# A fused attention and gated-MLP kernel: SyncE's transfers in the attention stage in written order, with new due times for the row maxima

## The chip, the cores and the metric

One Trainium2 chip, one NeuronCore of it. The metric is the device time of one execution in microseconds (us), as the median of several runs. The core has a matrix engine (TensorE, called PE in the profile, with its weight loads as PEld), two elementwise engines (VectorE, DVE; ScalarE, ACT), a slower general engine (GpSimd, POOL), and SyncE (SP), which here does nothing but issue DMA transfers. SBUF is the on-chip memory, PSUM holds matmul results, and DRAM tensors are off the core.

## The reference

`x` is 2048 by 576. Its normalised form goes through sliding-window attention (32 heads of 18, each query sees itself and the 255 keys before it); `x` itself goes through a gated MLP of width 4608 whose gate mixes positions by a 2048 by 2048 matrix.

```
def reference(x, wqkv, wo, x, w_in, w_sp, b_sp, w_out):
    qkv = layernorm(x) @ wqkv
    p = softmax(where(0 <= i - j < 256, q @ k.T * 18 ** -0.5, -1e9))
    s = (p @ v) @ wo
    z = gelu(x @ w_in);  z1 = z[:, :2304];  z2 = layernorm(z[:, 2304:])
    y = z1 * (w_sp @ z2 + b_sp[:, None])
    return x + s * silu(y @ w_out)
```

## The kernel before

Precision is kept by splitting a float32 operand into a high part (float32r) and the rest, and by multiplying three pairs of parts; most matmuls of the kernel are such triples.

The program has five stages, one after the other on PE. It normalises and transposes `x` and forms q and k (line 291). It forms v (458) and z2 (662). Then comes the attention stage, which this change concerns. After it follow the projection by `wo` (839), the mixing by `w_sp` (1029) and the output matmuls (1101).

The attention stage works in 16 units: 8 groups of four heads, first for the lower half of the queries (units 0 to 7), then for the upper half (units 8 to 15), which also see 256 keys of the lower half. Three kinds of work are interleaved on PE. First, `scores` (508) computes transposed scores of unit u, ACT takes the exponential (512), POOL cuts the window's edges (516, 519), and `pv` (532) multiplies by v, whose extra column of ones gives the softmax denominator. Second, `row_max` computes the row maxima of unit u+1, and of the first rows of unit u+2: a matmul (387) into one of two PSUM buffers `sp`, and a DVE instruction pair (391) that adds the window mask and reduces to the maximum. The maxima of a unit are written to DRAM (405) and read back as two more rows of q (409), so that the matmul for the scores subtracts them. Third, `z1_matmuls` (438) computes z1, which has nothing to do with attention and fills the gaps; its results go to DRAM by way of ACT (441) and a store (443), and each of its 18 weight blocks is loaded (416) and split by ACT and DVE (447) ahead of use.

`finish` ends a unit. The 4 by 1024 denominators are read out of `ou` into a 128 by 32 tile (`den`, 581), inverted on DVE (554), written to DRAM (556), read back spread over 32 rows for each head (`rp`, 559), and `ou` is multiplied by `rp` on DVE in two halves (567) and stored (576). So between the end of a unit and its store there is a chain: transfer, DVE, transfer, transfer, DVE, transfer.

The q and k of two heads share one slot tile of SBUF (`att0` to `att4`). `load_pair` fills a slot with eight transfers (346 to 349); at the start of unit u the pair for heads 2 and 3 of unit u+1 and the pair for heads 0 and 1 of unit u+2 are loaded. A row-maximum matmul reads the whole slot, so it needs all eight.

The order of the work is written out by a planner in the program itself. It keeps a running sum of estimated durations, `clock` (`spend`), and an estimate of when ACT and DVE come free (`use`, `busy`). `due` holds times at which each score block and each row maximum should be issued, as shares of the unit's length; where nothing is due, a z1 matmul is issued (`fill`). `after(ns, fn)` calls `fn` once the clock has gone on by `ns`; with it the planner places the steps of `finish`. `tc.manual_schedule` names the engines whose instructions run in exactly this order: before, PE, POOL, DVE and ACT in the attention stage. SP was not among them: the order of its transfers was chosen by the library's scheduler from dependences and its own time estimates. Whoever chooses it, SP issues in a fixed order: a transfer that waits holds back those behind it.

## Time and profile before

| what | value |
|---|---|
| median of 3 runs | 1983.74 us (1982.5 to 1984.1) |
| profiled execution | 1989.0 us |
| its span, first to last instruction | 1987.3 us |
| PE busy over the span | 1936.0 us, 97% |
| DVE / ACT / POOL busy | 1056.9 / 899.5 / 284.7 us |
| attention stage | about 448 to 987 us of the span |
| granted PE clock, mean | 0.995 |

All durations below come from the one profiled execution; the sum is made against its span. A busy PE in the profile means that a matmul is in the pipeline, so short gaps between matmuls do not show as idle; a stretch that does show as idle is a real halt of the stage, since PE works through its instructions in order. "Idle before, releaser" tells how long an engine had stood still ahead of an instruction and what ended it.

### The profile page before, as it was taken

Reading aid. Unit: us, or ns where it says so; the run is one execution under the profiler, and the core shown is the slowest. Engines: PE = TensorE matmul, PEld = TensorE weight load, DVE = VectorE, ACT = ScalarE, POOL = GpSimd, SP = SyncE. Lnnn points to the kernel's source line nnn. Section 1 sums busy time; section 2 is a strip of 40 time slices with the busy share of each in tenths; the row PEclk is TensorE's granted clock in tenths of the full one; section 3 lists DMA queues with packets and bytes.
Section 4 is the critical chain, followed back from the end, with each engine's and each line's share of the span. In section 5 each row is a group of like instructions: output and inputs, shape, how many; then the busy total and the mean of one; then the engine's idle time right before and its main releaser. Section 6 shows DMA issues by size and latency. Waiting matters only on the chain.

```text
span 1987.3 us, 30748 instructions
## 1 busy us (share of the span) xinstructions
PE 1936.0 (97%) x11096; PEld 1654.7 (83%) x11096; DVE 1056.9 (53%) x2294; ACT 899.5 (45%) x1673; POOL 284.7 (14%) x360
## 2 busy tenths in 40 slices
PE   6999999999999999999899999999999999999998
PEld 5889999996777777777697887788888888899998
DVE  6511233366666665655225768656876567653222
ACT  4222222215555555556546655655555534442121
POOL 5000365103222223223200000000000000000000
PEclk9999999999999999999999999999999999999999
DMA  8656799424455555454566757766667555865441
GB/s 248 174 146 170 253 344 338 173 82 138 130 153 147 155 140 153 138 149 112 159 224 219 249 187 257 270 212 217 217 224 258 178 181 183 266 211 164 138 147 56
DMA packets 221368, 375.58 MB, mean 189 GB/s; under 512 B 43296, under 2 KB 118176, under 8 KB 221088
## 3 DMA queue, kind: packets, MB, share of 16 engines
q1 hardware_dynamic: 205856, 349.66, 56.7%
q10 hardware_dynamic: 15360, 23.97, 3.3%
q8 instruction: 87, 1.43, 0.3%
q14 instruction: 65, 0.53, 0.1%
HBM read 260.45 MB, written 112.83 MB: 188 GB/s over the span
## 4 chain that ended last, share of the span: by engine, by line
PE 81%; DMA 10%; DVE 5%; issue 2%; ACT 1%; POOL 1%; SPq 0%; ACTq 0%; DVEq 0%; POOLq 0%
PE acc L1029 28%; PE po L1101 11%; PE mm L438 9%; PE mm L662 9%; PE mm L291 6%; PE sp L387 4%; PE ops L532 4%; PE tps L508 4%; PE wops L839 3%; PE vps L458 3%; DMA att<-st_d 2%; DMA z1t<-z_d 1%; DMA den<-ou 1%; DMA spr<-in_w_sp_dram 1%; DVE spl L112 1%
## 5 line engine op out<-in xcount | busy, mean ns | idle before, releaser
L1029 PE MATMUL acc<-spl,zh 128*128 128x512 f32 x1008 | 393.6, 390 | 2.9 <-DVE spl L112 2.7
L1029 PE MATMUL acc<-sph,zh 128*128 128x512 f32 x1008 | 393.3, 390 | 3.0 <-ACT sph L111 2.9
L1029 PE MATMUL acc<-sph,zl 128*128 128x512 f32 x1008 | 392.8, 390 | 0.0
L391 DVE CUSTOM_DVE_ANT_0 junk<-sp,band 128x384 bf16<-128x384 f32 (+1 forms) x512 | 269.1, 537 | 174.1 <-PE sp L387 168.1
L512 ACT ACTIVATE pt<-tps 128x384 f32<-128x384 f32 (+2 forms) x576 | 244.6, 438 | 191.5 <-PE tps L508 181.4
L438 PE MATMUL mm<-b,z1wh 128*128 128x512 f32 x648 | 236.0, 395 | 0.0
L1029 PEld LDWEIGHTS acc<-spl,zh 128*128 128x128 f32 x1008 | 189.6, 188 | 44.9 <-DVE spl L112 5.6
L1029 PEld LDWEIGHTS acc<-sph,zh 128*128 128x128 f32 x1008 | 189.5, 188 | 43.6 <-ACT sph L111 4.2
L112 DVE TENSOR_TENSOR spl<-spr,sph 128x1024 fp32r<-128x1024 f32 x168 | 205.3, 1222 | 36.6 <-ACT sph L111 35.5
L1029 PEld LDWEIGHTS acc<-sph,zl 128*128 128x128 f32 x1008 | 189.6, 188 | 39.2
L662 PE MATMUL mm<-z2wh,b 128*128 128x384 f32 x720 | 192.6, 337 | 2.2 <-ACT zt L672 2.2
L508 PE MATMUL tps<-att 128*128 128x384 f32 (+1 forms) x576 | 180.7, 324 | 8.7 <-ACT pt L512 8.7
L111 ACT ACTIVATE zh<-b 128x384 fp32r<-128x384 f32 x168 | 87.4, 520 | 221.6 <-PE acc L1029 221.5
L387 PE MATMUL sp<-att 128*128 128x384 f32 (+1 forms) x512 | 178.3, 354 | 8.1 <-DVE mx L391 4.1
L111 ACT ACTIVATE sph<-spr 128x1024 fp32r<-128x1024 f32 x168 | 175.9, 1047 | 6.4 <-DMA spr<-in_w_sp_dram 4.8
L112 DVE TENSOR_TENSOR zl<-b,zh 128x384 fp32r<-128x384 f32 x168 | 93.1, 554 | 148.2 <-ACT zh L111 147.8
L1101 PE MATMUL po<-b,yh 128*128 128x288 f32 x840 | 146.4, 296 | 0.0
L387 PEld LDWEIGHTS sp<-att 128*128 128x128 f32 x512 | 95.0, 188 | 61.6 <-issue 26.0
L438 PE MATMUL mm<-b,z1wl 128*128 128x512 f32 x360 | 142.4, 396 | 0.0
L673 DVE BATCH_NORM_STATS2 st<-zt 128x6 f32<-128x384 f32 x96 | 53.5, 559 | 166.1 <-ACT zt L672 166.0
L662 PE MATMUL mm<-z2wl,b 128*128 128x384 f32 x400 | 134.3, 336 | 0.0
L662 PEld LDWEIGHTS mm<-z2wh,b 128*128 128x128 f32 x720 | 131.4, 189 | 3.3 <-ACT zt L672 3.3
(154 smaller groups left out, 2852.9 us busy)
## 6 DMA issues: line engine op xcount, KB each, us to landing
spr<-sc_d SPq DMA_DIRECT2D x96, 512.0 KB
spr<-in_w_sp_dram SPq DMA_DIRECT2D x72, 512.0 KB
zr<-z_d SPq DMA_DIRECT2D x144, 192.0 KB
st_d<-qkhl SPq DMA_DIRECT2D x72, 256.0 KB
z_d<-zt ACTq DMA_DIRECT2D x48, 384.0 KB
z_d<-z1o SPq DMA_DIRECT2D x72, 256.0 KB
z1t<-z_d SPq DMA_DIRECT2D x72, 256.0 KB
y_d<-z1t SPq DMA_DIRECT2D x72, 256.0 KB
```

What stands on the lines that cost most here:

```text
L111: act.activation(hi, src, AF.Copy)
L112: dve.tensor_tensor(lo, src, f32(hi), ALU.subtract)
L291: pe.matmul(ps, w, r, start=n == 0, stop=n == len(pl) - 1)
L387: pe.matmul(ps[:, :w], q_of(u, j)[:, i * P:(i + 1) * P], k_of(u, j)[:, k0:k0 + w], start=True, stop=True)
L391: dve.tensor_tensor_reduce(out=junk[:, :w], in0=ps[:, :w], in1=band[:, m0:m0 + w], scale=1.0, scalar=-3.0e38, op0=ALU.add, op1=ALU.max, ac ...
L438: pe.matmul(ps, w, r, start=n == 0, stop=n == len(pl) - 1)
L508: pe.matmul(ps[:, :m * P], k_of(u, j)[:, (kb - base) * P:(kb - base + 1) * P], q_of(u, j)[:, (a - lo) * P:(a - lo + m) * P], start=True, s ...
L512: act.activation(pt[:, j, d0:d0 + n * P], ps[:, (qa - a) * P:(qa - a + n) * P], AF.Exp, scale=scale)
L532: pe.matmul(o_ps[c][32 * j:32 * j + 32, (lo - 4 * c) * P:(hi - 4 * c + 1) * P], vgs[u][:, kb - k0, j * VW:j * VW + 32], pt[:, j, (lo - kb) ...
L662: pe.matmul(ps[:, :ZW], r, wt, start=n == 0, stop=n == len(pl) - 1)
L1029: pe.matmul(acc[j], z[:, ps], w[:, cs], start=s == i == 0 and n in OPENS, stop=s == 7 and i == 2, skip_group_check=True)
L1101: pe.matmul(po[i][:, a, :288], y if ahead else y[:, i * P:(i + 1) * P], w[:, a * 288:(a + 1) * 288], start=f == 0 and m == 0, stop=f == NF ...
```

## The change

SP joins the engines in written order within the attention stage, and so every transfer there is now placed by the planner's clock:

- The sixteen transfers of the two pairs are issued one by one, 450 ns of the clock apart, from 300 ns after the start of the unit (in unit 0 4 us later). `load_pair` at once is still used ahead of attention.
- The steps of `finish`: `den` is read 300 ns after ACT's copy by the planner's account (before: 700 ns after the call); the reciprocal comes 5.5 us after the call (10 us); the write of the inverse follows it by 300 ns and the read of `rp` by another 2.7 us (before: at once, in this order); the first half is multiplied at 13.5 us (22.5), the second at 20.5 us (24.5), and the four stores follow 400 ns apart.
- The two transfers of the row maxima are placed 400 ns and 3 us after DVE's account is done; z1's store 200 ns after ACT's copy; z1's next weight block is loaded at the first matmul of a block instead of the fourteenth.
- Due times: the first 16 row maxima of a unit are spread up to 0.30 of its length and the others from 0.31 to 0.765 (before: all evenly to 0.74); 7 instead of 6 of the unit after next are taken in advance, from 0.81 on (0.78).
- Unit 0 gets a share of z1 matmuls of 24 against 18 (18.4 in the upper half), its scores and maxima are due 4 us later, and POOL clears both new slots, where DVE cleared one.
- The five blocks of `wo` pass through three buffers instead of two, and are split five score blocks later.

The diff, cut to its core:

```
-EARLY = 6
-RM2 = 0.78
-RM1 = 0.74
+EARLY = 7
+RM2 = 0.81
+RM1 = 0.765
+RMH = 0.30
 RMN = 33
 PVJ = 3
 PVN = 2
 NORM_AT = 2
 TAIL = 30
-_SHARE = [18 + 0.4 * (i >= 8) for i in range(16)]
+_SHARE = [18 + 0.4 * (i >= 8) + 6 * (i == 0) for i in range(16)]
...
-            def clear(i):
-                eng = (dve, pool)[i % 2]
+            def clear(i, eng=None):
+                eng = eng or (dve, pool)[i % 2]
...
-                    sp.dma_start(q[b:b + 36, :], st_d[0, 0:36, h, q0:q0 + HS])
-                    sp.dma_start(k[b:b + 18, :kn], st_d[1, 18:36, h, k0:k0 + kn])
-                    sp.dma_start(q[b + 36:b + 56, :], st_d[0, 18:38, h, q0:q0 + HS])
-                    sp.dma_start(k[b + 18:b + 54, :kn], st_d[1, 0:36, h, k0:k0 + kn])
+                    for dst, rows in ((q[b:b + 36, :], st_d[0, 0:36, h, q0:q0 + HS]),
+                                      (k[b:b + 18, :kn], st_d[1, 18:36, h, k0:k0 + kn]),
+                                      (q[b + 36:b + 56, :], st_d[0, 18:38, h, q0:q0 + HS]),
+                                      (k[b + 18:b + 54, :kn], st_d[1, 0:36, h, k0:k0 + kn])):
+                        sp.dma_start(dst, rows)
+                        loaded[p] = loaded.get(p, 0) + 1
+                        yield
...
                 def put_max():
                     sp.dma_start(m_d[u], f32(m))
+
+                def get_max():
                     rows = m_d[u].rearrange("(n j i) q -> n j (i q)", n=2, j=4)
                     for j in range(4):
                         b = 64 * (j % 2)
                         sp.dma_start(f32(q_of(u, j)[b + 54:b + 56, :]), rows[:, j])
 
-                after(500, put_max)
+                to_move[u] = [put_max, get_max]
+                wait = max(busy["dve"] - clock, 0) + 400
+                for ns in (wait, wait + 2600):
+                    after(ns, lambda: to_move[u] and to_move[u].pop(0)())
                 yield
...
-                                use("act", 620)
-                                sp.dma_start(z1_d[f * P:(f + 1) * P, cs], zo)
-                                if c == 0 and f + 1 < FH // P:
-                                    nxt = load_z1(f + 1)
+                                after(use("act", 620) - clock + 200,
+                                      partial(sp.dma_start, z1_d[f * P:(f + 1) * P, cs], zo))
+                            if n == c == 0 and f + 1 < FH // P:
+                                nxt = load_z1(f + 1)
...
                     dve.reciprocal(den, den)
-                    use("dve", 350)
-                    sp.dma_start(r_d[u].rearrange("h (a b) -> (h a) b", b=HS // 32), den)
+                    t = use("dve", 350) - clock + 300
+                    after(t if u < NU - 1 else 0,
+                          lambda: sp.dma_start(r_d[u].rearrange("h (a b) -> (h a) b", b=HS // 32), den))
+                    if u == NU - 1:
+                        tick()
+                    return t
...
                 def invert():
-                    put_inverse()
-                    get_inverse()
+                    after(put_inverse() + 2700, get_inverse)
...
-                    for i in range(4):
+
+                    def store(i):
                         h = 4 * g + i
                         sp.dma_start(o_d[h * DH:(h + 1) * DH, cs], ou[32 * i:32 * i + DH, :])
+
+                    for i in range(4):
+                        if u == NU - 1:
+                            store(i)
+                        else:
+                            after(busy["dve"] - clock + 200 + 400 * i, partial(store, i))
 
                 if u == NU - 1:
                     last.extend([lambda: sp.dma_start(den, ou[DH::32, :]), put_inverse, get_inverse, divide])
                 else:
-                    after(700, lambda: sp.dma_start(den, ou[DH::32, :]))
-                    after(10000, invert)
-                    after(22500, partial(divide_half, 0))
-                    after(24500, divide)
+                    after(busy["act"] - clock + 300, lambda: sp.dma_start(den, ou[DH::32, :]))
+                    after(5500, invert)
+                    after(13500, partial(divide_half, 0))
+                    after(20500, divide)
...
-                raw = wors[k % 2]
+                raw = wors[k % 3]
...
-                clear(i)
+                clear(i, pool)
...
-                heads.enter_context(tc.manual_schedule(engines=ENGINES | {ET.Activation}))
+                heads.enter_context(tc.manual_schedule(engines=ENGINES | {ET.Activation, ET.SP}))
...
-                spend(3000)
+                while to_move[0]:
+                    to_move[0].pop(0)()
...
-                busy.update(act=clock, dve=clock)
+                busy.update(act=clock + 4600, dve=clock + 4200)
...
-                    for p in (2 * u + 3, 2 * u + 4):
-                        if p < 2 * NU:
-                            load_pair(p)
+                    jobs = [(lambda it=it: next(it, None)) for p in (2 * u + 3, 2 * u + 4) if p < 2 * NU
+                            for it in [pair_jobs(p)] for _ in range(8)]
+                    for i, job in enumerate(jobs):
+                        after(300 + 450 * i + (4000 if u == 0 else 0), job)
...
-                    t0 = clock
+                    late = 4000 if u == 0 else 0
+                    t0, span = clock + late, span - late
+                    half_at, end_at = (RMH, RM1) if begun else (0.42, 0.84)
+                    when = [half_at * (n - begun + 0.25) / (16 - begun) if n < 16 else
+                            half_at + 0.01 + (end_at - half_at - 0.01) * (n - 16) / (RMN - 16) for n in range(begun, RMN)]
                     due = [[(t0 + span * (n + 0.5) / len(items), 0, n) for n in range(len(items))],
-                           [(t0 + span * (RM1 if begun else 0.84) * (n + 0.25) / nmax, 1, u + 1) for n in range(nmax)]
+                           [(t0 + span * f, 1, u + 1) for f in when[:nmax]]
...
-                        if u == NU - 1 and n % 5 == 1 and 2 <= n // 5 < 7:
+                        if u == NU - 1 and n % 5 == 1 and 3 <= n // 5 < 8:
```

How this moves the instructions. The first place is SP in unit 10, where unit 9 is finished (`den_8411` before, `den_8421` now; `att3` and `att4` are slots being loaded, `vg` is v for the next unit). Before:

```order
L348 DMA att4_4045<-st_d_60 20x1024
L349 DMA att4_4045<-st_d_60 36x1280
L443 DMA z1_d_64<-z1o_8395 128x512
L581 DMA den_8411<-ou_8224 128x1x32
L487 DMA vg_8506<-v_d_63 128x10x89
L416 DMA z1raw_8512<-in_w_z1_dram 128x640
L443 DMA z1_d_64<-z1o_8509 128x512
L556 DMA r_d_67<-den_8411 128x32
L559 DMA rp_8412<-r_d_67 128x1x1024
```

Now:

```order
L354 DMA att4_4040<-st_d_60 20x1024
L610 DMA den_8421<-ou_8238 128x1x32
L354 DMA att4_4040<-st_d_60 36x1280
L354 DMA att4_4040<-st_d_60 36x1024
L354 DMA att4_4040<-st_d_60 18x1280
L380 DMA z1_d_64<-z1o_8457 128x512
L576 DMA r_d_67<-den_8421 128x32
L506 DMA vg_8521<-v_d_63 128x10x89
L582 DMA rp_8422<-r_d_67 128x1x1024
```

The read of the denominators stood behind all sixteen loads of slots and a z1 store; now it stands behind eleven loads, with five behind it (three of them shown). The write of the inverse and the read of `rp` still follow one another, with `vg` now between them.

The second place is DVE at the same unit: the reciprocal, then the multiplication of the first half by `rp`, and what stands between (`junk` and `mx` are the pair of a row maximum, `mhl` its closing step). Before, eleven pairs and the closing step:

```order
L554 RECIPROCAL den_8411<-den_8411 128x32
L391 ISA junk_8555,mx_8248<-sp_8553,band_75 128x384
L391 ISA mx_8248 128x1
...
L391 ISA junk_8685,mx_8248<-sp_8683,band_75 128x384
L400 TENSOR_SCALAR mhl_8699<-sp_8697 32x128
L401 SCALAR_TENSOR_TENSOR mhl_8699<-sp_8697,mhl_8699 32x128
L567 TENSOR_TENSOR ou_8224<-ou_8224,rp_8412 128x512
```

Now, seven pairs:

```order
L573 RECIPROCAL den_8421<-den_8421 128x32
L405 ISA junk_8514,mx_8276<-sp_8512,band_75 128x384
L405 ISA mx_8276 128x1
...
L405 ISA junk_8583,mx_8276<-sp_8581,band_75 128x384
L589 TENSOR_TENSOR ou_8238<-ou_8238,rp_8422 128x512
L405 ISA junk_8604,mx_8276<-sp_8602,band_75 128x384
```

The multiplication came after the unit's last row maximum; now it comes in the middle of them, and more row maxima are queued behind it. At the ends of units 0 to 6, ten pairs stand between where thirteen stood.

The third place is POOL at the start of attention, the clearing of the new slots and the first cut of a window. Now:

```order
L637 TENSOR_TENSOR a11_3732<-a22_3738,a11_3732 128x512
L638 TENSOR_TENSOR a12_3734<-a12_3734,a11_3732 128x512
L327 MEMSET att3_4037 128x2048
L328 MEMSET att3_4037 128x1280
L327 MEMSET att4_4040 128x2048
L328 MEMSET att4_4040 128x1280
L535 AFFINE_SELECT pt_4096<-pt_4096 128x4x128
```

The two rows of `att4` stood on DVE before, between row maxima of unit 1.

More of the change, by code (lines that the diff above doesn't have):

```diff
@@ L803 @@
                     spend(MM)
-                clock += 100000
-                tick()
+                while waiting:
+                    clock += 100000
+                    tick()
             order.enter_context(tc.manual_schedule(engines=ENGINES | {ET.Activation, ET.SP}))
```

13 lines of the change are left out of this document (12 added, 1 removed).

## The prediction

> **What bounds the kernel now.** The page's first part and the busy time over the attention stage alone come first (columns of the second row: stretch and length, then PE, PEld, DVE, ACT and POOL busy, granted clock, DMA share, GB/s).
>
> ```profile
> PE 1936.0 (97%) x11096; PEld 1654.7 (83%) x11096; DVE 1056.9 (53%) x2294; ACT 899.5 (45%) x1673; POOL 284.7 (14%) x360
> 447.00:990.00 543.00, 523.85 (x3497) 391.36 (x3496) 313.80 (x1105) 317.42 (x742) 157.75 (x242) 1.00 0.53 142
> ```
>
> PE sets the end. In the stage that is changed it stands still for 543.0 - 523.9 = 19.2 us, and the change neither adds nor removes matmuls. So it can win at most those 19 us and what the clock loses by them. The waits of PE in that stretch say what they are (total, times, longest):
>
> ```profile
> PE tps L508 <- ACT pt L512: 8.7, 4, 3.1
> PE sp L387 <- DVE mx L391: 4.1, 6, 1.3
> PE sp L387 <- DMA att<-st_d: 2.2, 2, 1.3
> PE wops L839 <- ACT ohl L825: 2.0, 1, 2.0
> PE sp L387 <- DMA vg<-v_d: 1.6, 1, 1.6
> ```
>
> The timeline gives their places, and the rows by 20 us the clock after the one at 858:
>
> ```profile
> 452.98 0.45 PE L508 MATMUL tps<-att 128*128 128x384 f32 x1 [2.34 <-ACT pt L512]
> 456.17 0.44 PE L387 MATMUL sp<-att 128*128 128x384 f32 x1 [1.29 <-DVE mx L391]
> 857.48 0.42 ACT L447 ACTIVATE z1wh<-z1raw 128x256 fp32r<-128x256 f32 x1 [3.56 <-DMA z1raw<-in_w_z_dram]
> 858.33 0.69 PE L508 MATMUL tps<-att 128*128 128x384 f32 x1 [2.98 <-ACT pt L512]
> 974.36 0.68 ACT L111 ACTIVATE att<-wor 128x576 fp32r<-128x576 f32 x1 [3.42 <-DMA wor<-in_wo_dram]
> 975.37 0.39 PE L508 MATMUL tps<-att 128*128 128x256 f32 x1 [3.09 <-ACT pt L512]
> 840.00:860.00 20.00, 17.02 (x105) 13.66 (x105) 9.94 (x36) 10.08 (x26) 4.37 (x7) 0.95 0.74 182
> 860.00:880.00 20.00, 20.00 (x138) 14.17 (x137) 12.05 (x40) 10.89 (x26) 6.22 (x10) 0.97 0.30 97
> ```
>
> The pattern to see: ACT or DVE stands in its own queue before a transfer that has not landed, and PE, which needs a PSUM buffer back from that engine, stands behind. The same holds at the end of a unit. This is the chain of waits there (start, length, what):
>
> ```profile
> 782.04 5.31 DMA den<-ou
> 787.44 0.36 DVE den L554
> 787.82 4.02 DMA r_d<-den
> 791.86 8.45 DMA rp<-r_d
> 800.34 0.04 DVE ou L567
> 801.98 0.45 PE sp L387
> ```
>
> It is the chain that this change re-times, so its lengths decide.
>
> **The change part by part.** *What it removes.* At the start of attention, 2.34 + 1.29 = 3.6 us: the first scores are due 4 us later, with z1 matmuls in between, and DVE no longer clears a slot. The z1 block at 858: 2.98 us, and the clock, 20 x (0.05 + 0.03) = 1.6 us; the block's load is now issued thirteen matmuls earlier. The `wo` block at 975: 3.1 us, by the third buffer and five blocks more of distance. Late slot loads, 2.2 + 1.6 = 3.8 us (the wait put down to `vg` is at a row maximum, which reads slots): they are now in order, and the maxima that need them start at 0.31 of the unit. Sum -15.1 us. I take all of it; from below, only the first 3.6 us, where nothing but written order is involved. The other clearing goes to POOL, 2.9 us more before its first cut, which is itself due 4 us later: nothing. One more row maximum ahead moves work by one place, and 6 shares of z1 move into unit 0: the same matmuls, nothing. Sixteen issues spaced by 450 ns cost SP what they cost now.
>
> *What it adds: the read of `rp` comes too late.* The planner leaves 13.5 - 5.5 = 8.0 us between reciprocal and first multiplication, where it left 22.5 - 10 = 12.5. Its clock can be trusted at this point, as the first unit's rows show:
>
> ```profile
> 498.52 0.35 DVE L554 RECIPROCAL den<-den 128x32 f32<-128x32 f32 x1
> 498.90 0.32 SPq L556 DMA_DIRECT2D r_d<-den  x1
> 500.32 0.58 SPq L559 DMA_DIRECT2D rp<-r_d  x1
> 511.10 0.69 DVE L567 TENSOR_TENSOR ou<-ou,rp 128x512 f32<-128x512 f32 x1
> SPq L559 <- DMA r_d<-den: 27.5, 15, 3.6
> ```
>
> Planned 12.5, measured 511.10 - 498.52 = 12.58 us, without a wait. The two transfers between them do not get shorter by being placed closer. The write of the inverse: its issue 0.32 plus SP's mean wait of 27.5 / 15 = 1.83, so 2.2 us with the hand-over (1.42 here, 4.02 in the chain above). The read of `rp`: 8.45 in the chain. It takes that long even when little else moves:
>
> ```profile
> rp<-r_d SPq DMA_DIRECT2D x15, 512.0 KB
> 504.00:507.00 3.00, 3.00 (x22) 2.24 (x14) 2.10 (x8) 2.02 (x5) 0.88 (x2) 1.00 0.28 86
> 928.68 0.35 DVE L554 RECIPROCAL den<-den 128x32 f32<-128x32 f32 x1
> 931.60 0.57 SPq L559 DMA_DIRECT2D rp<-r_d  x1
> 940.55 1.29 DVE L567 TENSOR_TENSOR ou<-ou,rp 128x512 f32<-128x512 f32 x2 [0.18 <-DMA rp<-r_d]
> 990.66 0.35 DVE L554 RECIPROCAL den<-den 128x32 f32<-128x32 f32 x1
> 1003.14 1.29 DVE L567 TENSOR_TENSOR oul<-oul,att 128x512 f32<-128x512 f32 x2 [10.60 <-DMA att<-r_d]
> ```
>
> From 504 to 507 it is nearly alone, at 86 GB/s and a DMA share of 0.28: 512 KB need 6.0 us of that, to which at least 1 us goes for starting and landing (an estimate: it was issued at 500.32). From 931.60 it took 8.9 us. So the path from the start of the reciprocal is 0.4 + 2.2 + 8.5 = 11.1 us, at least 0.4 + 1.4 + 7.0 = 8.8, at most the chain's 800.34 - 787.44 = 12.9. DVE would be at the multiplication after 8.0 and wait 3.1 us (0.8 to 4.9).
>
> The Trainium skill, "DMA: Bandwidth & Descriptors", in the section on why a DMA increments its semaphore by 16, says that a transfer is spread over as many engines as divide the slowest dimension of both sides; `rp` is read as 4 by 32 by 1024, so by that rule over 4 of 16, and a share of 0.28 agrees. By the page's 27 GiB/s for an engine and 2.0 us of fixed cost it would take 6.5 us, the wait would be 1.1 us, and PE would lose next to nothing; the rows say 8.5.
>
> Behind the waiting multiplication are DVE's row maxima, behind them PE's matmul for the second next one (two `sp` buffers), and behind that everything on PE. How much of a DVE wait reaches PE can be read where it happened before:
>
> ```profile
> 752.94 0.35 DVE L554 RECIPROCAL den<-den 128x32 f32<-128x32 f32 x1 [1.54 <-DMA den<-ou]
> 753.77 0.44 PE L387 MATMUL sp<-att 128*128 128x384 f32 x1 [0.46 <-DVE mx L391]
> 787.44 0.35 DVE L554 RECIPROCAL den<-den 128x32 f32<-128x32 f32 x1 [1.82 <-DMA den<-ou]
> 788.27 0.44 PE L387 MATMUL sp<-att 128*128 128x384 f32 x1 [0.75 <-DVE mx L391]
> 800.34 1.11 DVE L567 TENSOR_TENSOR ou<-ou,rp 128x512 f32<-128x512 f32 x1 [1.10 <-DMA rp<-r_d]
> 801.98 0.45 PE L387 MATMUL sp<-att 128*128 128x384 f32 x1 [0.80 <-DVE mx L391]
> ```
>
> All but 1.08, 1.07 and 0.30 us. With 0.8 as the mean, 3.1 us on DVE are 2.3 us on PE. It happens after each of units 0 to 13 (unit 15, in which unit 14 is finished, has no row maxima): 14 x 2.3 = 32.2 us, between 0 and 14 x (4.9 - 0.3) = 64.
>
> *The reciprocal.* The read of the denominators is placed about 1 us after `finish` (ACT's copy and 300 ns), the reciprocal at 5.5: 4.5 us for a transfer that takes 5.3 in the chain above and 6.1 in another unit's:
>
> ```profile
> 681.88 6.13 DMA den<-ou
> ```
>
> It has eleven loads ahead of it still. DVE waits 0.8 to 1.6 us, or up to 2 if SP is late itself, of which 1.1 do not reach PE: I take 0.4 x 14 = 5.6 us, between 0 and 14 x 0.9 = 13. What stands there now, 0.46 + 0.75 + 0.80 = 2.0 us, is part of these terms and goes.
>
> *The clock.* Of the three longest halts above (2.34, 2.98, 3.09 us) one cost a slowed stretch, 1.6 us. For 14 halts of 2.3 us and more at the same odds: 14 / 3 x 1.6 = 7.5 us, between 0 and 22. The Trainium skill, "TensorE: Matmul & The Clock Gate", in the part on the HAM clock gate, gives a free-running window of 3.4 us, one idle window of which halves the clock; strictly read, no halt of 2.3 us would do it and this term would be nothing, but here 2.98 us did.
>
> *Sum.* 1987.3 - 15.1 - 2.0 + 32.2 + 5.6 + 7.5 = 2015.5 us of span, 28 more than before. The runs lie 3.6 us below the span (1983.7), so 2012.
>
> **The rivals.** *The transfer lands in time.* If SP, in clean order, gets `rp` off at once and it lands within about 8.8 us, nothing of the added terms remains and the runs are at 1983.7 - 17.1 = 1966.6. It decides from here: the added terms equal the gain of 17 when PE loses 1.2 us a unit, DVE 2.0, so at a path of 10.0 us. For it: the least of every piece adds up to less. Against it: the three places where DVE waited for this transfer measured 12.9, 11.9 (from the reciprocal at 928.68) and 12.5 (from 990.66, into `att`, in the next stage), and `vg` is now queued just ahead of `rp`. Chance 0.17, 1962 to 1979.
>
> *It does nothing that can be told* (a path near 10 us, or gains of only 3.6 us against small losses): 1980 to 1988. Within 0.2% of before, about what a measurement of this kernel can tell from no change, I give 0.06.
>
> *The queue behind the wait.* SP now stands at the write of the inverse until DVE has inverted, and `vg`, `rp`, z1's stores and its next weights wait behind it. With the path at its upper 12.9 us and every halt costing a clock stretch: 14 x 4.1 + 5.6 + 22 - 17 = 68 us, 2050. For it: SP already waited up to 3.6 us for r_d. Against it: PE's own halt gives those transfers time. Chance 0.15, 2035 to 2055.
>
> **How the numbers follow.** The forecast, DVE waiting for `rp` in nearly every unit, has 0.62, with its own range 1990 to 2035. Slower by over 0.2% then has 0.62 + 0.15 = 0.77, the same 0.06, faster 0.17. The range reaches into the first rival and to the middle of the last: 1974 to 2040 leaves out about 0.1 on each side.
>
> **What would show it.** In the profile after, DVE's idle time ahead of the multiplication, put down to `rp`, should be some 40 us (1.3 before), 2.5 to 4 us in a unit, and a PE halt at a row maximum should follow it within 2 us, with dents in the clock. The halts at 453, 858 and 975 should be gone. I am wrong if `rp` lands within 8 us of the reciprocal, or if PE finds other work while DVE stands.

## The result, and the profile after

The changed kernel takes 2061.05 us (median of 4 runs, 2058.8 to 2063.5) against 1983.12 us for the kernel before on the same chip: a ratio of 1.0394, with an interval from 1.0374 to 1.0413. It is 78 us slower. The forecast had it slower too, at 2012 us, and its range ended at 2040.

The mean granted clock and the busy time in the attention stage come first, as before. The span and the mean clock of the profiled executions, before:

```profile
core 0: 1987.3 us, clock 0.995
```

and after:

```profile
core 0: 2060.3 us, clock 0.978
```

The busy time of the changed kernel from 447 to 1062 us, which is now nearly the whole stage (columns as in the prediction):

```profile
447.00:1062.00 615.00, 549.40 (x3484) 413.04 (x3483) 313.23 (x1101) 314.29 (x738) 155.92 (x244) 0.93 0.46 123
```

PE stands still for 615.0 - 549.4 = 65.6 us of this stretch (19.2 before), and the granted clock is 0.93 (1.00 before). Over the spans, what the clock lost is 2060.3 x 0.022 = 45 us against 1987.3 x 0.005 = 10 us. The stage now ends at about 1064 us, and the span is 73 us longer. Some of the slowed stretches lie in the halts themselves. Counted only while PE is busy, the clock lost 34.5 us after and 8.3 us before; PE's idle time over the spans is 98.8 and 51.3 us. So the halts account for 47.5 us and the clock for 26 us, together the whole of the 73.

The waits of PE in the attention stage after (total, times, longest) have one large entry where there were several small ones:

```profile
PE sp L401 <- DVE mx L405: 64.3, 19, 6.8
PE tps L527 <- ACT pt L531: 0.7, 2, 0.4
PE sp L401 <- DMA att<-st_d: 0.4, 1, 0.4
```

What was removed is really gone: the waits of `tps` for ACT went from 8.7 to 0.7 us, those for slots from 3.8 to 0.4. Nearly all the rest is PE waiting for DVE at a row maximum (2.5 us are waits at the matmuls of `wo`, as good as unchanged). What DVE itself waits for:

```profile
DVE ou L589 <- DMA rp<-r_d: 67.7, 12, 8.9
DVE ou L589 <- issue: 13.3, 2, 8.4
DVE ou L589 <- DMA z_d<-z1o: 8.0, 1, 8.0
DVE den L573 <- DMA den<-ou: 17.3, 12, 3.0
```

The first three rows are the same wait, at the first multiplication by `rp`, in units 0 to 14; where the name is another, it is only what landed last by the record. Together they are 89 us, 1.3 before. The chain of waits at the end of unit 7 (the one shown of before is that of unit 9; start, length, what):

```profile
746.07 5.67 DMA den<-ou
751.76 0.36 DVE den L573
752.14 4.85 DMA r_d<-den
757.01 8.65 DMA rp<-r_d
765.78 0.69 DVE ou L589
...
767.00 0.69 PE sp L401
```

It has the same links as before, in about the same lengths (4.85 and 8.65 against 4.02 and 8.45). What differs is when DVE comes to the multiplication: there it had waited 1.10 us for the landing. The timeline of the same place says who stood still here:

```profile
751.76 0.35 DVE L573 RECIPROCAL den<-den 128x32 f32<-128x32 f32 x1 [1.87 <-DMA den<-ou]
752.59 0.44 PE L401 MATMUL sp<-att 128*128 128x384 f32 x1 [0.57 <-DVE mx L405]
765.78 0.69 DVE L589 TENSOR_TENSOR ou<-ou,rp 128x512 f32<-128x512 f32 x1 [8.89 <-DMA rp<-r_d]
767.00 0.69 PE L401 MATMUL sp<-att 128*128 128x384 f32 x1 [6.79 <-DVE mx L405]
```

DVE stood for 8.89 us, PE for 6.79. And the matmul that ended the halt took 0.69 us, where the same matmul took 0.44 at 752.59: it ran at the lower clock. An earlier halt, of 2.85 us, ends at 541.5; in the rows of busy time around it the third column from the end is the clock:

```profile
538.00:541.00 3.00, 0.68 (x6) 0.30 (x2) 0.70 (x2) 0.86 (x2) 0.58 (x1) 0.98 0.24 89
541.00:548.00 7.00, 6.47 (x18) 5.47 (x19) 3.21 (x12) 2.39 (x5) 1.22 (x2) 0.52 0.10 38
```

For nearly 7 us after the halt PE is busy at half clock: a z1 matmul takes 0.63 us in this stretch, and 0.40 us behind it.

### The profile page after: what moved, and what is told of

Same layout as the page of the kernel before. It is cut to its first block, busy times and chain, and to the rows that moved or that the text cites. A ratio compares the mean times of both kernels' runs of the same rounds, so it can differ in the third digit from the quotient of the medians.

```text
span 2060.3 us, 30742 instructions
## 1 busy us (share of the span) xinstructions
PE 1961.6 (95%) x11096; PEld 1675.2 (81%) x11096; DVE 1056.7 (51%) x2292; ACT 899.7 (44%) x1673; POOL 282.6 (14%) x362
## 4 chain that ended last, share of the span: by engine, by line
PE 73%; DMA 16%; DVE 5%; issue 3%; ACT 1%; POOL 1%; SPq 1%; DVEq 0%; ACTq 0%; POOLq 0%
PE acc L1070 27%; PE po L1142 11%; PE mm L691 8%; PE mm L457 7%; PE mm L292 5%; DMA rp<-r_d 5%; PE sp L401 3%; PE tps L527 3%; PE vps L477 3%; DMA den<-ou 3%; PE wops L880 3%; PE ops L551 2%; DMA r_d<-den 2%; DMA att<-st_d 1%; DMA z1t<-z_d 1%
## 5 line engine op out<-in xcount | busy, mean ns | idle before, releaser
L401 PE MATMUL sp<-att 128*128 128x384 f32 (+1 forms) x512 | 187.1, 370 | 64.7 <-DVE mx L405 64.3
L457 PE MATMUL mm<-b,z1wh 128*128 128x512 f32 x648 | 241.1, 411 | 0.0
L113 DVE TENSOR_TENSOR spl<-spr,sph 128x1024 fp32r<-128x1024 f32 x168 | 205.2, 1222 | 37.2 <-ACT sph L112 34.8
L401 PEld LDWEIGHTS sp<-att 128*128 128x128 f32 x512 | 101.4, 200 | 117.3 <-DVE mx L405 79.5
L527 PE MATMUL tps<-att 128*128 128x384 f32 (+1 forms) x576 | 193.1, 341 | 0.8 <-ACT pt L531 0.7
L457 PE MATMUL mm<-b,z1wl 128*128 128x512 f32 x360 | 147.9, 411 | 0.0
L535 POOL TENSOR_SCALAR_AFFINE_SELECT pt<-pt 128x512 f32<-128x512 f32 x128 | 83.7, 654 | 410.3 <-ACT pt L531 407.8
L527 PEld LDWEIGHTS tps<-att 128*128 128x128 f32 x576 | 114.5, 200 | 28.4 <-ACT pt L531 10.9
```

Source lines behind the costliest of these rows:

```text
L113: dve.tensor_tensor(lo, src, f32(hi), ALU.subtract)
L401: pe.matmul(ps[:, :w], q_of(u, j)[:, i * P:(i + 1) * P], k_of(u, j)[:, k0:k0 + w], start=True, stop=True)
L457: pe.matmul(ps, w, r, start=n == 0, stop=n == len(pl) - 1)
L527: pe.matmul(ps[:, :m * P], k_of(u, j)[:, (kb - base) * P:(kb - base + 1) * P], q_of(u, j)[:, (a - lo) * P:(a - lo + m) * P], start=True, s ...
L535: pool.affine_select(out=pt[:, :, 0:P], in_=pt[:, :, 0:P], pattern=[[0, 4], [1, P]], compare_op=ALU.is_ge, fill=0.0, base=0, channel_multi ...
```

## The experiments

The theory at this point, called A in the expectations: the whole loss is the multiplication by `rp`, placed ahead of the landing of `rp`, and the halts and the slower clock that follow from it. Its rivals: the written order of SP, the due times, or the row maxima queued behind the multiplication.

### Which part of the change costs

**The old times of the chain in the changed kernel, in two steps.** First only the halves of the multiplication go back, then the reciprocal too:

```
-                    after(13500, partial(divide_half, 0))
-                    after(20500, divide)
+                    after(22500, partial(divide_half, 0))
+                    after(24500, divide)
```

```
-                    after(5500, invert)
+                    after(10000, invert)
```

> The changed kernel with one thing undone: the two multiplications by the inverse are placed at 22.5 and 24.5 us after the end of a unit again (13.5 and 20.5 in the change); the reciprocal stays at 5.5, SyncE stays in written order, the new due times stay. Theory A, the loss is DVE waiting for the read of the inverse: the wait at the multiplication is gone, the halts at 453, 858 and 975 us stay away, only the waits for the denominators (17 us on DVE in all) are left; about 1972 us, 1962 to 1982. Theory B, the loss comes from SyncE in written order, which stands at the write of the inverse and holds back v, the z1 stores and the weights behind it, whatever DVE does: 2020 us or more. Theory C, the new due times of the row maxima cost by themselves: 2000 to 2060, with PE halts at row maxima that DVE's multiplication does not end.

> As the run with the late multiplications, and the reciprocal is placed at 10 us again (5.5 in the change). Theory A: the waits for the denominators go as well, 12 of them with 17 us on DVE, of which about a third reached PE; 1967 us, 1958 to 1978, and 0 to 8 us less than with the early reciprocal. Theory B: the write of the inverse stands in SyncE's queue just as before it, 2020 or more.

Measured: with the old halves 1985.0 us, ratio to before 0.9997 (0.9982 to 1.0011); with the whole old chain 1980.0 us, ratio 0.9969 (0.9953 to 0.9985). The loss of 78 us is gone in both. But each misses its expected number by 13 us, and its range: the gain of 15 us that the removed halts should bring is hardly there. With the old halves DVE and PE still waited here:

```profile
DVE den L573 <- DMA den<-ou: 29.4, 12, 3.7
PE sp L401 <- DVE mx L405: 10.5, 15, 2.3
```

With the whole old chain:

```profile
PE sp L401 <- DVE mx L405: 9.2, 11, 2.7
DVE ou L589 <- DMA rp<-r_d: 7.9, 3, 4.2
```

So old halts were replaced by new ones of about 10 us. What they come from is taken up below.

**The new times of the chain in the kernel before**, and nothing else of the change:

```
-                    after(10000, invert)
-                    after(22500, partial(divide_half, 0))
-                    after(24500, divide)
+                    after(5500, invert)
+                    after(13500, partial(divide_half, 0))
+                    after(20500, divide)
```

> The kernel before with one part of the change alone: reciprocal at 5.5, multiplications at 13.5 and 20.5 us after the end of a unit; the transfers are still ordered by the scheduler and the due times are the old ones. Theory A: DVE waits for the read of the inverse here too, some 5 us in a unit, with PE halts and a slowed clock after them; 2045 us, 2020 to 2075. Theory B and C: written order and due times are not there, so little is lost; 1980 to 1995.

Measured: 2058.7 us, ratio 1.0370 (1.0349 to 1.0392). Its waits (the lines are those of the kernel before):

```profile
DVE ou L567 <- DMA rp<-r_d: 53.2, 13, 6.7
DVE den L554 <- DMA den<-ou: 39.2, 12, 5.2
PE sp L387 <- DVE mx L391: 57.8, 25, 5.0
```

With SP left to the scheduler and the old due times, three numbers make the kernel as slow as the whole change does. Together with the two runs above this settles which part costs: the re-timed chain, alone. The written order of SP and the due times are neither needed for the loss nor do they soften it.

### What in the chain costs: its length or its place

**`rp` read as four transfers**, one for each head. The old read is 4 by 32 by 1024, and the prediction's rows had it at a DMA share of 0.28:

```
-                    sp.dma_start(rp, r_d[u].unsqueeze(1).to_broadcast([4, 32, HS]))
+                    for h in range(4):
+                        sp.dma_start(rp[32 * h:32 * h + 32], r_d[u, h:h + 1].to_broadcast([32, HS]))
```

> The changed kernel with the read of the inverse issued as four transfers, one for each head, instead of one over a leading dimension of four; the same bytes to the same places, so every transfer can go over more DMA engines. Theory A with the length of this transfer (8.3 us, at a DMA share of a quarter) as its main term: the transfer takes 3 to 5 us from the first issue, DVE's wait falls from 6 us in a unit to about 2, the halts and most slowed stretches of the clock go; 2000 us, 1980 to 2020. If the length is not set by its form but by what is queued ahead of it: it stays near 8 us and the time at 2050 to 2065. Theory B: no difference, 2050 to 2065.

Measured: 1989.8 us, ratio 1.0028 (1.0011 to 1.0045): 71 of the 78 us come back with every planned time left as it is. The waits:

```profile
DVE ou L590 <- DMA rp<-r_d: 31.8, 13, 4.3
PE sp L401 <- DVE mx L405: 17.9, 17, 2.2
```

DVE's wait for `rp` went from 89 to 33.1 us (1.3 of them under the name of another transfer), PE's from 64.3 to 17.9, and the mean clock is 0.995 again. The Trainium skill, "DMA: Bandwidth & Descriptors", section "Why a DMA increments its semaphore by 16 and not by 1", says that a transfer uses as many of 16 engines as divide its slowest dimension; the run agrees, since the same bytes in shapes with 32 in that place land about twice as fast. It is the shape and not the number of transfers, as the trace's records of single packets show. `rp` is 128 packets of 4 KB; of the one transfer, between 3.5 and 4.0 are under way on average in each of units 0 to 13. In the run below with four transfers and the first half at 16.5 us, the first of the four alone has 13 to 15 under way 0.3 us after its first packet (units 0, 1, 3 and 13, where no other packets of that size interfere); the second is issued 0.37 us behind it.

**A smaller dose: the first half at 16.5 us** instead of 13.5, with the one slow transfer:

```
-                    after(13500, partial(divide_half, 0))
+                    after(16500, partial(divide_half, 0))
```

> As the changed kernel, but the first half is multiplied at 16.5 us instead of 13.5. Theory A (the halts of the changed kernel are DVE's wait for rp less about 1.3 us, and a halt slows the clock only when it is long, since four-transfer rp left halts of 1 to 2 us with 6.8 us of half clock): DVE's wait falls by 3 us, from 67.7 + 13.3 + 8.0 over fourteen units to about 45 us, PE's halts to about 2 us each, the half clock from 85 us to below 30; median about 2005 us, 1997 to 2013. Rival P (the loss is proportional to DVE's wait, the clock with it): half of the 76 us stays, 2023 us or more. Rival N (3 us later is enough, because DVE would then come to the multiplication after the transfer): 1988 us or less.

Measured: 2017.2 us, ratio 1.0139 (1.0095 to 1.0183). The waits:

```profile
DVE ou L589 <- DMA rp<-r_d: 20.9, 8, 4.6
DVE ou L589 <- issue: 16.2, 6, 3.6
DVE ou L589 <- DMA z_d<-z1o: 4.4, 1, 4.4
PE sp L401 <- DVE mx L405: 27.7, 13, 4.4
PE sp L411 <- DVE mx L405: 7.1, 5, 2.3
```

DVE's wait is 41.5 us, near the 45 of theory A, and PE's halts are 34.8 us, 2.5 for each of fourteen units instead of 2; the time lies between A (up to 2013) and the proportional rival (2023). What A had too low above all is the clock, at a mean of 0.989: 2019.6 x 0.011 = 22 us lost, 12 more than before. I had taken halts of 2 us for harmless. Rival N falls: 3 us later is not enough.

**Both together**: the first half at 16.5 us and four transfers, by the two edits above.

> The changed kernel with the first half at 16.5 us and rp read as four transfers; the reciprocal stays at 5.5 us. With reciprocal to landing at 7.3 to 9.6 us no wait for rp is left against 11 us of distance. Theory A (only lateness matters, not where the multiplication stands): what remains are the waits for the denominators, as with the old times of the halves: 1985 us, 1981 to 1988, half clock near 0. Rival M (a multiplication in the middle of the row maxima costs by its place, since it puts 0.7 us between two maxima that PE's two buffers do not cover): 14 x 0.5 us more, 1990 us or above.

Measured: 1974.4 us, ratio 0.9944 (0.9918 to 0.9970), so faster than the kernel before. Its waits:

```profile
DVE den L573 <- DMA den<-ou: 21.7, 12, 3.2
PE sp L401 <- DVE mx L405: 3.9, 6, 1.4
DVE ou L590 <- DMA rp<-r_d: 0.6, 2, 0.4
```

and its timeline at the end of unit 8:

```profile
750.86 1.72 SPq L583 DMA_DIRECT2D rp<-r_d  x4
755.27 0.86 DVE L590 TENSOR_TENSOR ou<-ou,rp 128x512 f32<-128x512 f32 x1 [0.20 <-DMA rp<-r_d]
```

The four parts have landed 4.2 us after the first issue (755.07 - 750.86), against 8.65 for the one transfer in the chain above. The multiplication stands in the middle of the row maxima, as in the changed kernel, and costs nothing there: rival M falls, only lateness matters. And DVE still waits 21.7 us for the denominators, of which PE sees at most 3.9. That the time is 11 us below the expected one I had not foreseen. I had taken the 10.5 us of PE halts with the old halves as what the denominators cost. Read unit by unit, 7.5 of those 10.5 us do stand at the reciprocal, behind waits of DVE of up to 3.7 us. Here the waits are shorter, and PE's halts at the reciprocal come to 3.5 us. Why they are shorter no run shows.

### What a halt costs: the clock by itself

Two kernels were built on the last one, in which DVE does additional operations of no effect, the maximum of a part of `ou` with itself, in units 0 to 13: five in a row behind the first half's multiplication, or three there and three behind the second half's.

```
                     dve.tensor_tensor(ou[:, hs], ou[:, hs], rp[:, hs], ALU.mult)
                     use("dve", 750)
+
+                    for _ in range((5, 0)[a] if u < NU - 2 else 0):
+                        h0 = ou[:, :512]
+                        dve.tensor_tensor(h0, h0, h0, ALU.max)
```

with `(3, 3)[a]` in the second.

> The changed kernel with the first half at 16.5 us and rp in four transfers (1974 us, no wait for rp), in which DVE does five additional operations of 0.69 us in one row behind the first half's multiplication of units 0 to 13, each the maximum of a part of ou with itself, which changes nothing. With about 0.45 us of a DVE stall not reaching PE this is one halt of 3.0 us a unit. Halts above 2.6 us slowed the clock in nearly every unit so far, for one or two stretches of 3.4 us at half speed, which lose 1.7 us each. Theory A (the halt and the clock add): 1974 + 14 x 3.0 + 14 x 1.7 = 2040 us, 2030 to 2050, with at least ten slowed stretches. Rival Z (the clock's part is small, as the prediction had it): 2016 to 2024 us.

> As the run with one halt, but three additional operations behind the first half's multiplication and three behind the second half's, 4 us of the planner's clock later: six operations in all instead of five. Theory A (two halts of 1.6 us each lose as much idle time as one of 3.0, but are too short for the clock): 1974 + 14 x 3.2 = 2019 us, 2012 to 2026, with at most four slowed stretches, so 20 us faster than the run with one halt although DVE does 10 us more. Rival Q (the clock goes by the share of idle time, however it is cut, or the loss goes by DVE's work): as slow as the run with one halt, or slower.

Measured: five in a row 2048.4 us, ratio 1.0313 (1.0287 to 1.0340); three and three 2023.5 us, ratio 1.0187 (1.0172 to 1.0202). So six operations cost 25 us less than five. The mean clock and PE's waits with five in a row:

```profile
core 0: 2048.5 us, clock 0.982
```

```profile
PE sp L401 <- DVE mx L405: 36.5, 13, 4.3
PE sp L411 <- DVE mx L405: 16.7, 5, 3.4
```

With three and three:

```profile
core 0: 2021.0 us, clock 0.993
```

```profile
PE sp L401 <- DVE mx L405: 26.0, 22, 2.7
PE sp L411 <- DVE mx L405: 9.1, 7, 1.6
```

The clock lost 2048.5 x 0.018 = 37 us in the one and 2021.0 x 0.007 = 14 us in the other; PE's waits are 53.2 and 35.1 us. Rivals Z and Q fall. The cut into two groups was not quite what I had planned: the second group of three was mostly absorbed, so that the two kernels differ in idle time as well. Counted only while PE is busy, the clock lost 31 us in the one and 13 us in the other, and PE's idle time over the spans is 88 and 75 us. So of the 27.5 us between the spans the clock accounts for more than half (18 us), not for all.

The rows of busy time with three and three show both cases. A halt of 1.59 us lies in the first row, one of 2.67 us across the next two:

```profile
505.00:511.00 6.00, 4.41 (x24) 3.50 (x23) 5.38 (x14) 2.63 (x6) 1.93 (x2) 1.00 0.12 44
817.00:822.00 5.00, 2.89 (x15) 2.29 (x13) 4.23 (x9) 3.02 (x7) 1.22 (x2) 1.00 0.30 111
822.00:826.00 4.00, 3.43 (x35) 2.18 (x35) 3.67 (x11) 0.56 (x2) 1.34 (x2) 0.57 0.00 0
```

After the short one the clock stays at 1.00, after the longer one it is near half.

### Why the write of the inverse was slow

In the changed kernel the write of the inverse took 4.85 us in the chain shown, where the forecast had 2.2. Suspected were the slot loads that SP issues ahead of it. The last eight of the sixteen were put 12 us later:

```
-                        after(300 + 450 * i + (4000 if u == 0 else 0), job)
+                        after(300 + 450 * i + 12000 * (i >= 8) + (4000 if u == 0 else 0), job)
```

> The changed kernel with the last eight of the sixteen slot loads of each unit issued 12 us later, so that only eight stand ahead of the chain. It tells whether these loads are what made the write of the inverse slow (3.6 us instead of the forecast 2.2) and the denominators late. Theory A: the write lands after about 2 us, the reciprocal waits less than 0.5 us, the path from reciprocal to rp is about 11 us as forecast; DVE's wait goes down by 1 to 2 us a unit; median 2040 us, 2020 to 2050. Rival R (the write is slow because of z1 stores, v and weights, or because it is written in pieces of 128 bytes): within 6 us of 2061.

Measured: 2053.5 us, ratio 1.0340 (1.0318 to 1.0362), outside the range of A and just outside that of R. The write did get faster: SP's wait for it fell from the first of these rows (the changed kernel)

```profile
SPq L582 <- DMA r_d<-den: 35.9, 15, 4.1
```

to this one (late loads):

```profile
SPq L582 <- DMA r_d<-den: 8.9, 13, 1.4
```

But the loads now go out right behind the read of `rp`, as the timeline of this kernel shows (the second row is SP issuing eight loads),

```profile
871.60 0.54 SPq L582 DMA_DIRECT2D rp<-r_d  x1
872.19 10.34 SPq L354 DMA_DIRECT2D att<-st_d  x8
```

and the read takes longer, by its chain of waits:

```profile
871.60 10.62 DMA rp<-r_d
```

Over units 0 to 13 the write went from 3.7 to 1.9 us on average (from the end of the reciprocal to the issue of the read) and the read from 8.4 to 10.8 us (from its issue to the multiplication). So A was right about the cause of the slow write, and wrong in expecting the path to get shorter: what the write gained the read lost. The loads cost the chain its time at both places tried.

### Where the gain of the removed halts went

**Old chain and four transfers** in the changed kernel, by the edits shown above:

> The changed kernel with all three old times of the chain (reciprocal at 10 us, halves at 22.5 and 24.5) and with rp read as four transfers of one head each. Theory A: the 7.9 us that DVE still waited for rp with the old times go, and the part of PE's 9.2 us at the row maxima that follows them; the transfer is over about 3.5 us sooner and nobody waits for it. Median 1976 us, 1973 to 1980, against 1980 with one transfer. Rival: the wait for rp in the upper half is SP's own lateness with the write of the inverse, which four issues do not mend, or the faster transfer takes room from the loads: 1980 us or more.

**Four transfers in the kernel before**, by the same edit and nothing else:

> The kernel before, with nothing changed but the read of rp as four transfers. It tells whether the 10 us that the changed kernel with its old chain and four transfers wins over the kernel before come from the transfer or from written order and due times. Theory A (before, DVE waited only 1.3 us for rp in all, so nobody needs it sooner; the halts at 453, 858, 921 and 972 us stay): 1982 us, 1978 to 1985. Rival S (the transfer over 4 engines delays the other transfers on them, and that is what cost, as four transfers gave 6.5 us with the old chain): 1977 us or less.

**Old chain and the old due times of the row maxima** in the changed kernel, with one transfer (beside the edits to the chain):

```
-EARLY = 7
-RM2 = 0.81
-RM1 = 0.765
+EARLY = 6
+RM2 = 0.78
+RM1 = 0.74
...
-                    half_at, end_at = (RMH, RM1) if begun else (0.42, 0.84)
-                    when = [half_at * (n - begun + 0.25) / (16 - begun) if n < 16 else
-                            half_at + 0.01 + (end_at - half_at - 0.01) * (n - 16) / (RMN - 16) for n in range(begun, RMN)]
+                    end_at = RM1 if begun else 0.84
+                    when = [end_at * (n + 0.25) / nmax for n in range(nmax)]
```

> The changed kernel with the three old times of the chain and the old due times of the row maxima (even to 0.74, six in advance from 0.78); SP in written order, unit 0, the new weights and the third buffer stay. It tells where the expected gain of 15 us went, of which the old chain alone returned about 5. Theory D (the tighter due times of the first sixteen maxima make new short halts at them, some 0.6 us a unit): 1974 us, 1970 to 1977. Rival S (SP's written order holds the write of the inverse behind the loads, whatever the due times): no better than 1980 us, and DVE's wait for rp stays at 8 us. Rival L (without the new due times the slot loads come late again): 1984 us or more, with PE waits on slot loads.

Measured: old chain and four transfers 1973.5 us, ratio 0.9922 (0.9893 to 0.9952); four transfers in the kernel before 1978.1 us, ratio 0.9973 (0.9958 to 0.9988); old due times 1986.0 us, ratio 1.0002 (0.9983 to 1.0021). PE's waits at the row maxima with the old chain and four transfers:

```profile
PE sp L401 <- DVE mx L405: 3.0, 7, 0.5
```

The 9.2 us of short halts that stood there with one transfer are down to 3.0. Of the 9.2, 6.2 us are four halts right behind a wait of DVE for `rp`, in units 7, 9, 10 and 12, and these four are gone, as theory A had it. This version beats both kernels, the kernel before by 10 us by the medians and by about 15 us by its ratio. The transfer alone gives 0.27% in the kernel before, the rest of the change with the old chain 0.31%, both together 0.78%; the intervals are 0.3 to 0.6 points wide, so the sum of the first two cannot be told from the third. The time of the first, 1978.1 us, lies at the lower end of A's range and above S's 1977, so neither is confirmed; by the ratio the slow `rp` cost the kernel before something too, though DVE's own waits for it were 1.3 us.

With the old due times the short halts at DVE go, but others come, the longest at the slots:

```profile
PE sp L401 <- DMA att<-st_d: 7.9, 5, 3.0
```

The short halts that theory D named are gone, but its time was not reached; rival L holds, the loads are late once more, though SP is in written order. The time alone would suit rival S as well, but DVE's waits for `rp` are down to 5.2 us, where S had them stay near 8. SP's written order does not bring them in time by itself; the new due times are needed for it.

## Why the prediction was right or wrong

**The sign and the mechanism were right.** PE halts at a row maximum behind DVE, DVE stands at the multiplication, `rp` has not landed, once in each of the fourteen units. The kernel before with only the new times is as slow as the changed one, and four transfers at the same times undo 71 of the 78 us.

**What the change removes: the halts went, the time only in part.** Forecast -15.1 and -2.0. The halts that were to go are gone, 8.7 to 0.7 and 3.8 to 0.4 us. But with the old chain and one transfer only some 6 us of time showed, because short halts of 9.2 us came in their place, most of them still behind `rp`. Where no late `rp` is left, the spans are 1971.8 (old chain, four transfers) and 1972.6 us (16.5 us, four transfers) against 1987.3, which is 15 us; but part of that is the four transfers' own, since they gave 0.27%, some 5 us, in the kernel before.

**The step that failed first: "DVE would be at the multiplication after 8.0 and wait 3.1 us (0.8 to 4.9)".** Read unit by unit in the trace, DVE waited 3.7 to 8.9 us in these fourteen units, 5.9 on average. Of the 2.8 us that are missing, 1.2 are the path, which took 12.3 us on average instead of 11.1, nearly all of it in the write of the inverse (3.6 on average instead of 2.2; the run with late loads shows that the loads ahead of it cause this). The read itself was as forecast, 7.5 to 9.1 us. The other 1.6 us are DVE's arrival: after 6.5 us, not 8.0. The reciprocal was late by its own wait for the denominators, 1.2 us on average and 1.87 us in the row shown, while the work behind it came up in time, so DVE had less than the planned distance to do between the two. The prediction had counted the late reciprocal as a loss of its own, and left the planned 8.0 us behind it unchanged. This is most of it but not all. With the late loads the reciprocal waits nowhere in these units, and DVE arrives after 8.4 us in units 0 to 6 but after 6.5 us in units 7 to 13. So the planner's clock, which the prediction trusted from the rows of the first unit, is off by about 1.5 us in the later ones of that run.

**The PE halts.** Of PE's 64.3 us at row maxima, about 62 belong to these fourteen places, 4.4 each, where 2.3 were forecast. The part that does not reach PE was 1.5 us, larger than the 0.8 taken; this error made the forecast higher, not lower. The waits at the reciprocal cost 2.2 us of PE halts in all, against a term of 5.6.

**The step that left its bounds furthest: "The clock", 7.5 us, between 0 and 22.** Measured 45 - 10 = 35 us. The odds of one halt in three came from three halts, and were applied to halts of 2.3 us; the halts were twice as long, and all fourteen were followed by a slowed stretch. The three halts were also a matter of luck, by where each of them fell; the last section shows how. By these sizes the sum is 1987.3 - 17.1 + 62 + 2 + 35 = 2069, 9 us above the span of 2060.3: halts that fall into a slowed stretch are counted in both terms.

**The rivals.** `rp` does not land in time as one transfer, and as four it does only with the first half at 16.5 us or later. The third rival, a path of 12.9 us with every halt costing a clock stretch, was the nearest at 2050: its path and its rule for the clock came true. Its mechanism, transfers held up in SP's queue behind the wait, did not: all but 3.6 us of PE's waits in the stage are for DVE at a row maximum. It also let one stretch of 1.6 us follow each halt, where most had two.

## What to carry to other kernels

Before a step that waits for a chain of transfers is placed earlier, add up the chain as it will be with the neighbours that its queue will have, and if it does not fit, make the transfer shorter: here splitting a 512 KB broadcast into four was worth 71 us, and moving the step gained nothing that shows (1974.4 us with the first half at 16.5 us, 1973.5 at its old place). Count the distance from where the waiting engine will really stand, since a late step upstream eats the planned distance of the next one. A halt of the matrix engine in every iteration has two prices, its length and the clock after it, and for halts of mostly 3 us and more the second was about half as large as the first.

## What the hardware did that I had not expected

**How long a halt may be before the clock falls.** In the attention stages of the fourteen profiled kernels (before, after and the experiments) there are 186 halts of PE above 0.4 us; the trace also records the stretches at half clock, which come in multiples of 3.41 us. Counted by the length of the halt:

| halt, us | halts | no slowed stretch | one of 3.41 us | two or more |
|---|---|---|---|---|
| 0.4 to 1.7 | 93 | 93 | 0 | 0 |
| 1.7 to 2.3 | 17 | 10 | 7 | 0 |
| 2.3 to 2.9 | 21 | 4 | 14 | 3 |
| 2.9 to 3.5 | 23 | 8 | 9 | 6 |
| 3.5 to 4.2 | 18 | 0 | 5 | 13 |
| above 4.2 | 14 | 0 | 2 | 12 |

Halts below 1.7 us never did it, halts above 3.5 us always did. Between them equal halts go both ways: with five additional operations, three halts of 3.35 us left the clock alone and two more of the same length did not. The traces show what decides. In each of the fourteen executions all slowed stretches begin on one grid with a step of 3.413 us, over the whole execution; in the changed kernel, those that begin at 506.76, 540.90 and 578.45 us are 10 and 11 steps apart. The attention stages (from 447 us on) were cut into the windows of this grid, and PE's idle time was added up in each window that lies wholly in the stage:

| clock in the window | PE idle in it, us | windows | half clock in the next |
|---|---|---|---|
| full | below 1.7 | 2073 | 0 |
| full | 1.7 to 1.8 | 9 | 0 |
| full | above 1.8 | 72 | 71 |
| half | up to 0.52 | 71 | 0 |
| half | 0.57 and more | 35 | 35 |

So it is not the length of a halt that counts in these runs but how much of it falls into one window, with a border near 1.8 us, about half the window. The three halts on which the prediction based its odds show it in the kernel before. The halt of 2.98 us that ended at 858.33 put 2.49 us into the first of these windows, and the clock fell at its end; the halt of 3.09 us that ended at 975.37 was split between the other two, 1.61 and 1.48 us, and the clock stayed (the halt of 2.34 us at 453 left no window with more than 1.51 us):

```profile
854.43:857.84 3.41, 0.92 (x5) 0.48 (x3) 1.01 (x5) 0.36 (x2) 0.00 (x0) 1.00 1.01 280
970.48:973.89 3.41, 1.80 (x9) 1.18 (x7) 0.00 (x0) 0.46 (x1) 1.23 (x2) 1.00 0.40 155
973.89:977.31 3.42, 1.94 (x19) 0.88 (x19) 1.96 (x3) 1.96 (x5) 0.65 (x1) 1.00 0.02 6
```

That is a count over traces that were there; no run shifted a halt against the grid on purpose. The Trainium skill, "TensorE: Matmul & The Clock Gate", section "Why this matters for your kernels", advises to avoid gaps above about 3 us; in these runs gaps from 1.7 to 2.9 us were followed by half clock in 24 of 38 cases, so the measurement asks for about half of that.

**What four transfers gave where hardly anybody waited for `rp`.** Four transfers instead of one made the kernel before faster by 0.27% although DVE had stood there for no more than 1.3 us. Who had been waiting is not settled: the profiled execution of that run took 1984.9 us, the longest of the ten, so its halts do not tell. In the changed kernel with the old chain it is clear: there DVE itself still waited for `rp` in four units, as told above. That the one transfer also holds up its neighbours is possible, and no run shows it.
